# A hand-fixed issue order replaced by another: the same operations of an adaptive-norm, local-attention and token-mixer block in a different sequence, with other engines for some norms

## The chip, the core and the metric

The kernel runs on one core of a Trainium2 chip. The core has a matrix engine (PE, with its weight loads shown separately as PEld), a vector engine (DVE), a scalar engine for activations (ACT), a general engine (POOL) and a queue engine (SP) that issues the DMA transfers. Every engine works through its own list of instructions in the order in which they were issued and stops at the first one whose inputs are not there. The metric is the device time of one execution in microseconds (us). The kernel before takes 211.51 us, the median of three runs between 209.7 and 211.93.

## What is computed

One transformer-like block on `x` of 2048 rows by 512 columns, in bf16. A condition vector `c` gives six rows of 512 (shift, scale and gate for each half). The first half is a layer norm with shift and scale, a local dilated attention (32 heads of width 16; each row sees 8 rows at distance 0, 2, ... 14) and a projection. The second half is two layer norms in sequence and an MLP that mixes along the 2048 rows, not along the columns.

```python
def _A_ref(x, wqkv, wo):                     # H = 32 heads of 16, W, dil = (8, 2)
    qkv = (x @ wqkv) ...                     # q, k, v
    idx = pos[:, None] - off[None, :]        # rows s, s-2, ... s-14
    logits = jnp.einsum('bhsd,bhswd->bhsw', q, kg) * scale
    attn = _softmax(jnp.where(mask, logits, -1e9))
    return jnp.einsum('bhsw,bhswd->bhsd', attn, vg) ... @ wo
def _B_ref(x, w1, b1, w2, b2):               # F = 1792
    h = _layernorm(x)
    u = _gelu(jnp.einsum('bsd,sf->bdf', h, w1) + b1)
    return (jnp.einsum('bdf,fs->bds', u, w2) + b2) transposed
sa, ca, ga, sb, cb, gb = (silu(c) @ w_mod) in six rows
h = _layernorm(x) * (1 + ca) + sa
x = x + ga * _A_ref(h, A_wqkv, A_wo)
h = _layernorm(x) * (1 + cb) + sb
x = x + gb * _B_ref(h, B_w1, B_b1, B_w2, B_b2)
```

## The kernel before

The 2048 rows are 16 tiles of 128. They are worked in five chunks of 2, 4, 4, 4 and 2 tiles. The program first describes every operation (its engine or a choice of engines, what it reads and writes, which buffer it takes and frees), and then issues all of them in the order of one long list of names, `ORDER`. A name may carry a suffix: `:a`, `:d`, `:p` choose ACT, DVE or POOL where there is a choice, and `:q` makes a matrix operation issue its matmuls in four pieces of 32 output columns each:

```python
    def schedule(self):
        ...
        for pos, token in enumerate(ORDER.split()):
            name, *rest = token.split(":")
            if name == "fill":
                k, n = map(int, rest)     # n matmuls of 128 columns into a free bank
                ...
            o = by_name.pop(name)
            o.quad = rest == ["q"]
            assert all(d in done for d in o.deps), name
            for eng, dur, fn in o.alts:
                if rest and eng[0] == rest[0]:
                    o.eng, o.dur, o.fn = eng, dur, fn
    ...
    def mm(out, lhsT, rhs, **kw):
        if not G.quad:
            return nc.tensor.matmul(out, lhsT=lhsT, rhs=rhs, **kw)
        for j in range(0, P, 32):
            nc.tensor.matmul(out[j:j + 32], lhsT=lhsT[:, j:j + 32], rhs=rhs, tile_position=(0, j), **kw)
```

The names that matter, with `c` for a chunk and `t` for a tile:

- `ln1s t`, `rstd1_c`, `nb1_c`, `n1_t`: statistics (DVE), reciprocal deviation (ACT), bias (DVE) and the normalised tile of the first norm. `n2_t` and `h3_t` are the same for the second and third norm. Which engine does `n1_t`, `n2_t`, `h3_t` is letter `t` of the three strings `NE`.
- `wsc`: the weights of q, k, v scaled by the condition; `hT` and `xt t`: the transposed tile, by PE and a copy in the first two chunks, by a transposing DMA in the last three; `qkv c_..`: its projection; `ev`: the copy of the result out of PSUM.
- `qk c_d`: products of q and k (DVE), `red c_d`: their sum over a head (PE), `max`, `sub`, `exp`, `esum`, `rcp`, `smB`: softmax; `a2_c`: a DMA that spreads the weights, `vd c_d`: a DMA that spreads v; `pv c_d`: products of weights and v (DVE), `pvacc c_d`: their sum (PE), `oev`: its copy.
- `wo t`, `x1_t`, `ln2q t`, `ln2m`, `aff`, `ln3s`: projection, residual, sums for the second norm, shift and scale, statistics of the third.
- `mlp1_l_f_s`: first mixer product of feature tile `f` over some row tiles from `s`, `park`, `padd`, `gelu`: storing or adding a partial sum, activation; `mlp2_t` and `fin t`: second product and the output tile; `ld_`, `st_`: transfers.

The softmax and value part of one chunk, as code (cut):

```python
        for dlo in range(4):
            s_ = _Slot("big")
            ...
            add("dve", _t_tt2(NW * C), f, ..., alloc=s_, locks=True, name=f"qk{ch}_{dlo}")
            ...
            add("pe", ..., f, reads=["consts", "big_use"], frees=s_, writes=["psL"],
                name=f"red{ch}_{dlo}", tiled=True)
        ...
                add("dve", _t_tt2(8 * C), f, reads=[("a2sb", ba, jj) for jj in range(4)] + [("vD", ch, dq)],
                    frees=s_v, alloc=s_p, locks=True, name=f"pv{ch}_{dq}")
```

There are four `big` buffers, five `vD` buffers (`NVD: int = 5`) and six PSUM banks. The choice of engine for a normalised tile is made here:

```python
        alts = {"A": ("act", 0.8, lambda: nc.scalar.activation(dst, src, ACT.Identity, scale=r_, bias=n_)),
                "D": ("dve", 0.42, lambda: nc.vector.tensor_scalar(dst, src, args[0], args[1], op0=args[2], op1=args[3])),
                "P": ("pool", 0.8, lambda: nc.gpsimd.tensor_scalar(dst, src, args[0], args[1], op0=args[2], op1=args[3]))}
        G.add_any([alts[e]], reads=reads, writes=writes, name=name, locks=True)
```

The small numbers in these calls belong to the program's own planning; they are not measurements.

Of the kernel before, what the change touches and what calls it, by code (L numbers as in the profile page):

```python
# [182 lines left out]
act_table ld_x_1_2 ident ld_x_1_4 ld_x1 ld_c consts warm2 ld_x_4_14 ld_x0 ld_wmod1 ld_wqkv1 ln1s3 halo0 ld_x_2_8
fill:1:11 cps ln1s4 ld_x_2_6 ln1s1 ln1s2 ln1s0 ld_wqkv0 ln1s5 rstd1_0 silu_exp nb1_0 rstd1_1 n1_1 n1_0 silu_dve
ld_wmod0 ln1s15 ld_x_3_10 fill:2:83 modcols1 tr0_0 nb1_1 a1col ln1s14 n1_4 n1_5 ld_wqkv2 wsc1_3:a wsc1_2:d n1_3
hT0_2:d hT0_1:d hT0_3:a ln1s9 wsc1_1:a n1_2 ld_x_3_12 ln1s6 wsc1_0:a ld_wo3 fill:4:39 tr1_0 hT0_0:a tr1_2 ln1s7
hT1_0:a ld_wmod3 qkv0_10 wsc0_3:a wsc0_0:d ld_wmod4 hT1_1:d qkv0_12:q ln1s8 wsc0_1:a hT1_3:d rstd1_2 modcols0
wsc0_2:d ev0_12:d qkv0_00 sab nb1_2 hT1_2:d n1_6 n1_8 qvb0 n1_7 ln1s10 qkv0_02 rstd1_4 ev0_10:a wsc2_3 nb1_4
qvb_cp0 ln1s11 qkv1_10 ev0_00:a wsc2_2 ln1s13 qkv1_00 wsc2_1:a qk0_0 ev0_02:a qvb1 qkv1_12 wsc2_0:a qvb_cp1
qk0_1 ev1_10:a qkv0_22 qk0_3 qkv0_20 ev0_22:a red0_0 qk0_2 ev1_00:a xt6 qkv1_01:q ev0_20:a qk1_0 qkv1_02:q  # L190
ld_wmod2 n1_9 red0_1 vd0_0 halo_v1:a red0_2 ev1_02:a red0_3 mask qkv1_21:q ev1_12:a xt9 max0 ev1_01:a qkv1_11:q
qk1_2 ev1_21:a vd0_1 sub0:q qkv1_03:q ev1_11:a vd0_3 exp0 qkv1_13 xt7 qk1_1 esum0 ev1_13:a qkv1_22 xt8 rcp0
ev1_03:a modcol2 smB0 qkv1_20 qk1_3 a2_0_1 qkv1_23 a2_0_2 ev1_20:a a2_0_0 n1_15 red1_0 a2_0_3 red1_1 ln1s12
ev1_22:a red1_2 ld_wo1 mcols0 red1_3 rstd1_3 vd0_2 qkv2_00 nb1_3 max1 mrowt0 n1_10 n1_12 qkv2_10 ev1_23:a xt10
pv0_0 ev2_00:a qkv2_03 n1_13 pv0_3 vd1_3 qkv2_01 ev2_10:a vd1_2 n1_11 sub1 qk2_0 qkv2_12 exp1 xt11 qkv2_11
ev2_01:a ld_b2 pvacc0_0 mrows0:a pv0_2 ev2_11:a esum1 xt12 qkv2_13 rcp1 qk2_1 ev2_12:a qkv2_23 vd1_0 ev2_03:a
xt13 qkv2_20:q ev2_13:a ev2_23:a smB1 pvacc0_2 halo_k3:a qkv2_21:q qk2_3 a2_1_2 qkv2_02:q a2_1_0 red2_0 ev2_02:a
red2_1 a2_1_3 pv0_1 halo_v2:a pvacc0_3 ev2_21:a qkv3_11:q a2_1_1 st_row0 oev0_2:a ld_wo2 qk2_2 qkv3_00:q
ev2_20:a vd1_1 qkv3_02:q ld_wo0 qkv2_22:q ld_row0 ev3_02:a pv1_3 n1_14 red2_2 red2_3 ev2_22:a xt14 pvacc0_1
qkv3_01:q max2 qkv3_10:q ld_b1 ld_wmod5 pv1_1 qkv3_20:q ev3_10:a vd2_3 ev3_01:a sub2:q vd2_1 ev3_20:a qkv3_13:q  # L200
exp2 pv1_2 vd2_2 qkv3_21:q xt15 esum2:q ev3_21:a oev0_0:a qkv3_12:q pv1_0 vd2_0 ev3_13:a pvacc1_3 ev3_12:a woq_s
qkv3_23:q ev3_00:a rcp2 qkv3_22:q ev3_11:a pvacc1_2 ev3_23:a qk3_1 wo1:q pvacc1_0 x1_1 wo0:q smB2 qkv4_20:q
qk3_0 a2_2_2 oev1_3:a halo_v3:a a2_2_1 oev1_2:a pvacc1_1 a2_2_0 qkv3_03:q oev1_1:a oev1_0:a a2_2_3 qk3_2 modcol3
x1_0 ld_w1_0_512 ev3_03:a wo2:q ev4_20:a qk3_3 ln2q1 wo3:q ev3_22:a red3_0 vd3_3 x1_3 red3_1 mcols1 pv2_0 wo5:q
ln2q0 x1_2 mrowt1 wo4:q ln2q2 ln2m0 mrows1:a pv2_1 qkv4_22:q ln2q3 st_row1 vd3_0 rstd2_0 red3_2 x1_4 red3_3
warm3 ev4_22:a nb2_0 max3 n2_0 pvacc2_0 n2_1 ld_row1 qkv4_00 vd3_2 ln2m2 ln2q4 pv2_3 sub3 ld_w1_0_896 rstd2_2
pvacc2_1 exp3 x1_5 esum3:q pv2_2 ev4_00:a qkv4_02 oev2_1:a qkv4_10:q ln2q5 aff0 rcp3 pvacc2_3 oev2_0:a pvacc2_2
nb2_2 ev4_02:a smB3 qkv4_12 n2_2 ln2m4 a2_3_0 ln3s0 oev2_3:a oev2_2:a ld_w1_0_0 n2_3 ln3s1 ev4_10:a a2_3_1 wo8
halo_v4:p aff2 rstd3_0 a2_3_2 rstd2_4 wo9 a2_3_3 ev4_12:a nb3_0 nb2_4 wo7 x1_8 ln3s2 n2_5 vd4_2 warm0 n2_4 ln3s3
h3_1 ld_w2_0 aff4 rstd3_2 vd3_1 biascols h3_0 warm1 wo6:q nb3_2 biascols_cp:d ln3s4 h3_3 h3_2 x1_7 ln3s5  # L210
mlp1_0_5_0:q pv3_0 ld_w2_2 mlp1_0_2_0:q ln2q8 ln2q7 mlp1_0_6_0:q rstd3_4 x1_6 mlp1_0_0_0:q nb3_4 pv3_3 vd4_1
h3_5 mlp1_0_1_0:q h3_4 x1_9 mlp1_0_0_4:q mlp1_0_1_4:q pv3_2 vd4_3 park0_0:a pvacc3_3 mlp1_0_2_4:q park0_1:a
mlp1_0_3_0:q park0_2:a mlp1_0_3_4:q pv3_1 pvacc3_2 ln2q9 oev3_3:a ld_w1_0_1152 mlp1_0_4_0:q vd4_0 ln2q6 pvacc3_0
oev3_2:a mlp1_0_4_4:q qk4_2 oev3_0:a pvacc3_1 mlp1_0_6_4:q ld_w2_3 oev3_1:a ln2m6 mlp1_0_5_4:q qk4_0 park0_3:a
wo12:q rstd2_6 park0_4:a nb2_6 qk4_1 wo10:q n2_8 n2_7 n2_9 wo13:q ld_w1_0_1408 qk4_3 n2_6 red4_0 park0_5:a
red4_1 aff6 wo11:q x1_12 x1_13 red4_2 red4_3 x1_11 mlp1_0_10_0:q x1_10 max4 mlp1_0_9_0:q ln2q11 ln3s6 sub4:q
mlp1_0_7_0 ln3s7 exp4 ln2q12 ln3s8 esum4 mlp1_0_8_0 ln3s9 rcp4 park0_6:a mlp1_0_11_0 smB4 rstd3_6 ln2m11 a2_4_2
ln2q13 h3_7 mlp1_0_12_0 h3_6 a2_4_0 ln2m12 mlp1_0_10_4 h3_9 rstd2_12 a2_4_3 nb2_12 h3_8 a2_4_1 mlp1_0_8_4 n2_12
ln2m13 aff12 mlp1_0_8_8 rstd2_13 mlp1_0_11_4 ln2q10 nb2_13 ln3s12 n2_13 mlp1_0_7_4 ln2m10 pv4_0 rstd2_10
mlp1_0_7_8 rstd3_12 mlp1_0_9_4 ld_w1_0_1664 park0_7:a pv4_2 mlp1_0_9_8 park0_8:a mlp1_0_10_8 nb2_10 pv4_3  # L220
mlp1_0_11_8 n2_10 ld_w1_1_0 mlp1_0_12_4 rstd2_11 pv4_1 park0_9:a mlp1_0_12_8:q park0_10:a pvacc4_2 ld_w1_1_640
pvacc4_0 aff13 pvacc4_3 park0_11:a mlp1_0_13_0:q oev4_2:a ln3s13 inj1_2:q park0_12:a pvacc4_1 mlp1_0_13_4 nb2_11
aff10 rstd3_13 n2_11 ld_w2_5 oev4_0:a nb3_13 mlp1_0_13_8 wo14 nb3_12 ln3s10 aff11 rstd3_10 wo15 h3_12 x1_14
h3_13 inj1_1 ln3s11 inj1_4 mlp1_1_4_6 x1_15 ld_w1_1_896 inj1_3 mlp1_1_3_6 nb3_10 ln2s15 inj1_0 mlp1_1_0_6 h3_10
ln2s14 rstd2_15 rstd3_11 rstd2_14 n2_15 park0_13:a mlp1_1_1_6 aff15 mlp1_1_0_10 n2_14 mlp1_1_3_10 mlp1_1_4_10
park1_0:a nb3_11 ln3s15 mlp1_1_2_6 h3_11 aff14 mlp1_1_1_10 rstd3_15 mlp1_1_2_10 inj1_6 mlp1_1_6_6 nb3_15
ld_w1_1_1408 ln3s14 h3_15 mlp1_1_6_10 park1_1:d rstd3_14 inj1_5 mlp1_1_5_6 h3_14 park1_2:a mlp1_1_5_10 park1_3:d
mlp1_1_10_10 ld_w1_2_0 park1_4:a mlp1_1_8_10 park1_5:d park1_6:a mlp1_1_9_10 ld_w2_1 mlp1_1_12_10 mlp1_1_7_10
padd1_12 padd1_10 gelu12 mlp1_2_4_11 ld_w1_2_640 padd1_7 gelu10 mlp1_2_4_14 padd1_9 gelu7 mlp1_2_1_11 padd2_4
mlp1_2_2_11 ld_w2_7 padd1_8 mlp1_2_2_14 mlp1_2_3_11 gelu8 gelu4 mlp1_2_3_14 mlp1_2_0_11 padd2_3 mlp1_2_6_11  # L230
padd2_2 gelu3 gelu2 mlp1_2_0_14 padd2_6 mlp1_2_1_14 padd2_0 mlp1_2_5_11 padd2_1 mlp1_2_5_14 gelu0 mlp1_1_13_10
ld_w2_9 padd2_5 gelu1 gelu6 mlp1_1_11_10 gelu5 padd1_13 gelu13 mlp2_0_0 padd1_11 gelu9 gelu11 mlp2_0_0b mlp2_1_0
ld_w2_11 mlp2_0_0c fin1_0 mlp2_2_0 ld_w2_4 st_out1_0 mlp2_6_0 fin2_0 mlp2_5_0 mlp2_9_0 fin5_0 st_out5_0
st_out2_0 ld_w2_13 mlp2_7_0 fin9_0 fin6_0 mlp2_3_0 st_out6_0 mlp2_4_0 fin3_0 fin0_0 st_out3_0 st_out9_0
mlp2_13_0 st_out0_0 fin4_0 mlp2_8_0 fin7_0 st_out7_0 mlp2_10_0 st_out4_0 ld_w2_15 mlp2_11_0 fin10_0 fin13_0
fin8_0 mlp2_12_0 st_out13_0 fin11_0 st_out8_0 st_out10_0 st_out11_0 mlp2_14_0 fin12_0 st_out12_0 mlp2_15_0
fin14_0 mlp2_15_1 st_out14_0 fin15_0 mlp2_15_2 fin15_1 st_out15_0 st_out15_1 fin15_2 st_out15_2
"""


# [777 lines left out]
```

## Time and profile before

| | before |
|---|---|
| median of three runs | 211.51 us |
| span of the profiled execution | 208.9 us |
| PE busy | 196.4 us, 2208 matmuls |
| DVE busy | 165.3 us, 262 instructions |
| ACT busy | 113.8 us, 264 instructions |
| POOL busy | 16.9 us, 41 instructions |
| DMA moved | 35.99 MB |

Read "busy" as the time in which an instruction of the engine was under way. For PE that is generous: matmuls overlap in a pipeline, and one of 512 columns is listed with 379 ns while such matmuls start 0.22 us apart. All issues go through helpers, so the profile puts nearly all of them on one source line (L133), and instructions have to be told apart by the tiles they write and read: `big<-q_sb,k_f` is `qk`, `big<-a2sb,vD` is `pv`, `psS<-h,wst` is `mlp1`, `psS<-gT,...` is `mlp2`, `psL<-big,group` is `red`, `hT<-h` is a transposing DMA.

### The profile page before, as it was taken

To read this page: it belongs to the slowest core of one execution; us is meant where nothing else is said; L and a number is where in the kernel's file an instruction comes from. 1 tells how busy PE (TensorE), PEld (TensorE's weight loads), DVE (VectorE), ACT (ScalarE), POOL (GpSimd) and SP (SyncE) were. 2 spreads that over 40 slices of the span, in tenths; PEclk is the share of its full clock that TensorE was granted. 3 is DMA by queue.
4 is the path that set the end of the run, shared out by engine and by line. 5 is a ranking of instruction groups with operands and counts; after the bars stand their busy time and mean duration, and the time that the engine had idled before them with its cause. 6 is when DMAs were issued, how large, how long until landed. Compare 5 with 4: busy or idle time off the path is not lost.

```text
span 208.9 us, 5321 instructions
## 1 busy us (share of the span) xinstructions
PE 196.4 (94%) x2208; PEld 110.4 (53%) x2208; DVE 165.3 (79%) x262; ACT 113.8 (54%) x264; POOL 16.9 (8%) x41
## 2 busy tenths in 40 slices
PE   7999999995999898997899999999999999999993
...
DVE  3999999799999899999999999992771416370964
...
GB/s 165 341 369 259 22 199 163 175 237 140 205 155 291 153 217 263 147 230 292 122 259 136 19 78 310 232 109 246 227 348 109 28 0 119 132 75 141 25 100 52
DMA packets 55115, 35.99 MB, mean 172 GB/s; under 512 B 24628, under 2 KB 52404, under 8 KB 55092
## 3 DMA queue, kind: packets, MB, share of 16 engines
...
q10 hardware_dynamic: 8, 0.00, 0.0%
...
## 4 chain that ended last, share of the span: by engine, by line
PE 52%; DVE 28%; DMA 7%; ACT 5%; issue 4%; SPq 3%; DVEq 0%
PE psS L133 50%; DVE big L133 11%; DVE st L133 6%; DVE h L133 5%; DMA hT<-h 3%; SPq L133 3%; PE psL L133 3%; DVE mv L133 3%; DMA woq<-in_A_wo_dram 2%; DMA xx<-in_A_x_dram 2%; ACT xx L133 1%; DVE lsb L133 1%; ACT q_sb L133 1%; DVE nb L133 1%; DVE hT L133 1%
## 5 line engine op out<-in xcount | busy, mean ns | idle before, releaser
L133 PE MATMUL psS<-h,wst 128*32 128x512 bf16 (+1 forms) x392 | 51.5, 379 | 2.0 <-ACT h L133 1.6
L133 PE MATMUL psS<-hT,w_qkv 128*32 128x512 bf16 (+3 forms) x588 | 46.9, 346 | 4.0 <-DMA hT<-h 3.4
L133 PEld LDWEIGHTS <-wst 128*128 128x128 bf16 (+1 forms) x494 | 29.8, 98 | 31.8 <-issue 4.1
L133 PEld LDWEIGHTS <-w_qkv 128*32 128x32 bf16 (+1 forms) x630 | 31.3, 109 | 23.4 <-issue 7.1
L133 DVE TENSOR_TENSOR big<-a2sb,vD 128x4096 bf16<-128x4096 bf16 (+1 forms) x20 | 36.5, 1859 | 1.2 <-DMA a2sb<-lsb 1.0
L133 DVE TENSOR_TENSOR big<-q_sb,k_f 128x4096 bf16<-128x4096 bf16 (+1 forms) x20 | 36.7, 1856 | 0.7 <-ACT q_sb L133 0.7
L133 DVE SCALAR_TENSOR_TENSOR h<-psS,bcol,rows_bc 128x512 f32<-128x512 f32 (+2 forms) x18 | 12.4, 689 | 23.6 <-PE psS L133 23.5
L133 PE MATMUL psS<-gT,big 128*128 128x512 bf16 x112 | 24.5, 379 | 0.0
L133 PEld LDWEIGHTS <-ident 128*128 128x128 bf16 (+1 forms) x315 | 16.2, 104 | 6.5 <-issue 1.9
L133 PEld LDWEIGHTS <-big 128*128 128x128 bf16 x144 | 12.0, 97 | 13.8 <-issue 0.6
L133 POOL TENSOR_SCALAR h<-xx,rs,nb 128x512 bf16<-128x512 bf16 x12 | 10.0, 834 | 111.9 <-DVE nb L133 110.9
L133 PE MATMUL psS<-woq,o_sb 128*32 128x512 bf16 (+1 forms) x196 | 16.7, 380 | 0.6 <-ACT o_sb L133 0.6
L133 ACT ACTIVATE lv<-mv,epscol 128x1 f32<-128x1 f32 (+2 forms) x25 | 7.3, 290 | 16.1 <-DVE mv L133 14.6
L133 DVE BATCH_NORM_STATS2 st<-xx 128x6 f32<-128x512 bf16 x18 | 12.1, 673 | 3.7 <-DMA xx<-in_A_x_dram 3.6
L133 DVE TENSOR_TENSOR psS<-psS,gT 128x512 f32<-128x512 f32 x14 | 9.1, 695 | 6.9 <-PE psS L133 6.9
L133 ACT ACTIVATE q_sb<-psS,qvb 128x512 bf16<-128x512 f32 (+1 forms) x20 | 11.6, 601 | 4.5 <-PE psS L133 3.9
L133 PE MATMUL psS<-ident 128*128 128x128 bf16 x169 | 12.4, 240 | 1.4 <-POOL epscol L133 1.4
L133 ACT ACTIVATE h<-xx,nb,rs 128x512 bf16<-128x512 bf16 x14 | 11.2, 811 | 3.3 <-DVE nb L133 3.3
L133 ACT ACTIVATE v_sb<-psS,qvb 128x512 bf16<-128x512 f32 (+1 forms) x20 | 11.6, 605 | 1.9 <-PE psS L133 1.8
L133 DVE TENSOR_TENSOR h<-h,xx 128x512 bf16<-128x512 f32 (+2 forms) x18 | 11.4, 633 | 1.6 <-DMA out_dram<-h 0.9
L133 ACT ACTIVATE gT<-psS,bcol 128x512 bf16<-128x512 f32 x14 | 8.9, 686 | 6.6 <-DVE psS L133 6.5
L133 DVE TENSOR_TENSOR h<-h,rows_bc 128x512 bf16<-128x512 bf16 (+2 forms) x20 | 12.2, 608 | 0.4
...
## 6 DMA issues: line engine op xcount, KB each, us to landing
...
```

Of the source, the lines that this page charges most:

```text
L133: r = fn(*a, **k)
```

## The change

The list `ORDER` is replaced by another list of the same operations, and the three strings `NE` by others. No operation is added or taken away apart from the filler matmuls (133 before, 129 after). What the list moves or re-assigns, cut to its core:

```diff
-fill:1:11 cps ... fill:2:83 modcols1 tr0_0 ... fill:4:39 tr1_0 tr1_2 ... qkv0_10
+cps ... fill:2:108 tr1_0 ... tr0_0 modcols1 ... tr1_2 ... fill:0:21 qkv0_12
-wsc1_3:a wsc1_2:d wsc1_1:a wsc1_0:a wsc0_3:a wsc0_0:d wsc0_1:a wsc0_2:d wsc2_1:a wsc2_0:a
+wsc1_3:a wsc1_2:a wsc1_1:d wsc1_0:d wsc0_3:d wsc0_0:a wsc0_1:d wsc0_2:d wsc2_1:a wsc2_0:d
-hT1_1:d hT1_3:d ev0_12:d biascols_cp:d halo_v1:a halo_v2:a halo_v4:p park1_1:d park1_2:a park1_4:a park1_5:d
+hT1_1:a hT1_3:a ev0_12:a biascols_cp:a halo_v1:p halo_v2:d halo_v4:a park1_1:a park1_2:d park1_4:d park1_5:a
 # queue order around chunk 2 and 3 (only some names)
-xt11 ld_b2 xt12 vd1_0 xt13 a2_1_2 a2_1_0 a2_1_3 a2_1_1 st_row0 ld_wo2 vd1_1 ld_wo0 ld_row0
+ld_wmod4 xt12 xt13 vd1_2 a2_1_1 xt11 a2_1_0 a2_1_2 a2_1_3 xt14 vd1_3 st_row0 ld_b1 ld_wo3 ld_wo0 ld_row0
-ld_wmod5 vd2_3 vd2_1 vd2_2 xt15 vd2_0
+vd2_1 vd2_3 ld_b2 vd2_0 ld_w1_0_0 xt15 vd2_2
 # suffix :q (four pieces) on 60 matrix operations before, 44 after:
-qkv 25, sub 3, esum 2, wo 11, mlp 18, inj 1
+qkv 12, sub 3, wo 13, mlp 16
-    NE=('PDPPAPADPAAAPAAA', 'PAPPAPAAADAPDPDD', 'APPAAADDDDPPAADA'),
+    NE=('PAAPAPAADPAAAAPA', 'APAPAPAAADADDPPA', 'APPAAADDDDDDDPAD'),
```

It is meant to let the engines wait less for each other: work that another engine needs soon goes earlier, and tiles go to the engine that is less pressed at that place. The built programs agree with the list: the PE list has 4002 entries instead of 4418, mostly because fewer operations are issued in four pieces, and the DVE list fills 244 rows instead of 251 (equal neighbours share a row there).

More of the change, by code (lines that the diff above doesn't have):

```diff
@@ L182 @@
 ORDER = """
[L183 to L237, printed above, removed]
+ld_x_1_2 ld_c ident act_table ld_x_1_4 ld_x_2_8 consts warm2 ld_x1 ld_x0 cps ld_x_4_14 ld_wmod1 ln1s3 ld_wqkv1
@@ new lines @@
+ln1s4 ld_x_2_6 ld_wqkv0 ln1s5 ln1s2 ln1s0 rstd1_1 nb1_1 ln1s1 n1_4 n1_3 ld_wmod0 ln1s9 silu_exp rstd1_0 n1_5
+n1_2 nb1_0 ln1s14 n1_0 n1_1 ld_x_3_10 fill:2:108 tr1_0 silu_dve halo0 ld_wqkv2 hT1_1:a ln1s8 tr0_0 modcols1
+hT0_0:a hT0_2:d tr1_2 hT0_1:d hT0_3:a a1col wsc1_2:a wsc1_0:d ld_x_3_12 wsc1_1:d wsc1_3:a ln1s7 hT1_0:a
+fill:0:21 qkv0_12 ln1s6 ld_wmod2 wsc0_0:a wsc0_1:d qkv0_10 ld_wmod3 wsc0_2:d wsc0_3:d hT1_3:a ln1s15 qkv0_00
+rstd1_2 nb1_2 hT1_2:d ld_wmod5 n1_9 n1_6 modcols0 n1_8 qkv1_10 ld_wo1 sab ev0_10:a ln1s10 ev0_12:a qvb0 ln1s11
@@ new lines @@
+qkv0_02 wsc2_3 qvb_cp0 wsc2_0:d ev0_00:a qvb1 ln1s13 wsc2_2 qkv1_12 wsc2_1:a qvb_cp1 qk0_1 qkv1_00 ev0_02:a
+qk0_0 ev1_10:a qkv0_22 qkv0_20 ev0_22:a qk0_3 qkv1_02 ev1_00:a xt6 qk0_2 ev0_20:a red0_0 qkv1_01:q rstd1_4 qk1_0
+halo_v1:p vd0_0 ev1_02:a red0_1 red0_2 vd0_3 red0_3 ev1_12:a mask qkv1_11 ev1_01:a xt8 max0 qkv1_22 ev1_11:a
+qk1_2 n1_7 xt9 sub0 qkv1_03 ev1_22:a qkv1_13 exp0 xt7 qk1_1 esum0 ev1_13:a qkv1_23 vd0_2 ev1_03:a rcp0 qkv1_21
+ld_wo2 ev1_23:a vd0_1 smB0 modcol2 qk1_3 ev1_21:a a2_0_2 qkv1_20 a2_0_3 red1_0 ev1_20:a a2_0_1 red1_1 red1_2
@@ new lines @@
+a2_0_0 nb1_4 mcols0 ln1s12 n1_14 n1_15 red1_3 vd1_1 qkv2_10 max1 rstd1_3 qkv2_01 ev2_10:a halo_v2:d nb1_3 pv0_3
+n1_10 qkv2_00 ev2_01:a xt10 pv0_2 qkv2_11 ev2_00:a sub1 n1_13 qk2_0 vd1_0 qkv2_23 ev2_11:a ld_wmod4 n1_12
+qkv2_03 exp1 xt12 qkv2_13 qk2_1 ev2_03:a esum1 xt13 qkv2_12:q rcp1 ev2_13:a mrowt0 smB1 pvacc0_2 n1_11 vd1_2
+qkv2_02:q qk2_3 ev2_12:a a2_1_1 pvacc0_3 red2_0 halo_k3:a xt11 ev2_02:a qkv2_20:q ev2_23:a qkv2_21 qk2_2 a2_1_0
+a2_1_2 qkv2_22:q ev2_21:a a2_1_3 ev2_20:a red2_1 xt14 pv0_1 oev0_2:a red2_2 qkv3_10 ev2_22:a pv0_0 mrows0:a
@@ new lines @@
+vd1_3 qkv3_21 st_row0 pv1_2 qkv3_01 ld_b1 ld_wo3 red2_3 ld_wo0 qkv3_02:q pv1_0 qkv3_00 ev3_21:a pvacc0_0 ld_row0
+pvacc0_1 qkv3_03 vd2_1 oev0_0:a pv1_3 vd2_3 qkv3_13 ev3_03:a ld_b2 ev3_01:a qkv3_23 vd2_0 max2 ld_w1_0_0
+qkv3_12:q ev3_23:a xt15 woq_s sub2:q ev3_12:a pvacc1_3 ev3_00:a vd2_2 pvacc1_0 pv1_1 ev3_10:a wo0:q ev3_02:a
+wo1:q x1_0 qk3_0 ev3_13:a pvacc1_1 oev1_3:a pvacc1_2 exp2 qkv3_11 oev1_1:a qk3_3 esum2 oev1_2:a modcol3 rcp2
+oev1_0:a red3_0 x1_1 smB2 qkv3_20:q ev3_11:a qk3_2 a2_2_0 ln2q1 wo5:q a2_2_2 ev3_20:a a2_2_3 wo4:q x1_5 a2_2_1
@@ new lines @@
+mcols1 halo_v3:a qk3_1 qkv3_22:q ln2q0 ld_w1_0_896 x1_4 wo3:q ev3_22:a mrowt1 ln2m0 x1_3 red3_1 pv2_1 red3_2
+rstd2_0 wo2:q mrows1:a ln2q5 st_row1 ln2q3 red3_3 nb2_0 pv2_0 n2_1 qkv4_02 x1_2 ln2q4 qkv4_20:q ld_row1 ev4_02:a
+qkv4_00 vd3_2 max3 ev4_20:a ld_w1_0_512 pvacc2_1 pv2_3 n2_0 warm1 ev4_00:a sub3:q qkv4_22:q exp3 pv2_2 pvacc2_3
+ln2q2 pvacc2_0 esum3 halo_v4:a ld_w2_4 oev2_3:a qkv4_10 vd3_0 rcp3 ln2m4 ln2m2 oev2_0:a pvacc2_2 aff0 rstd2_2
+biascols oev2_2:a oev2_1:a nb2_2 smB3 n2_3 n2_2 wo8 ln3s0 a2_3_1 ev4_22:a ln3s1 a2_3_3 warm3 rstd2_4 a2_3_2
@@ new lines @@
+wo6:q aff2 rstd3_0 vd4_0 x1_8 qkv4_12:q a2_3_0 biascols_cp:a nb3_0 ev4_10:a nb2_4 ln3s3 n2_5 n2_4 ld_w2_1 wo9:q
+ln3s2 h3_1 vd3_3 h3_0 aff4 vd3_1 warm0 rstd3_2 x1_6 wo7:q nb3_2 ln3s5 h3_3 h3_2 x1_7 ln3s4 mlp1_0_6_0:q ev4_12:a
+pv3_0 mlp1_0_1_0:q rstd3_4 ln2q7 mlp1_0_5_0:q ln2q8 mlp1_0_2_0:q nb3_4 pv3_2 vd4_3 h3_4 mlp1_0_0_0:q h3_5 x1_9
+mlp1_0_0_4:q mlp1_0_1_4:q pv3_3 vd4_1 park0_0:a mlp1_0_6_4:q pvacc3_2 park0_1:a mlp1_0_2_4:q ln2q6 mlp1_0_3_0:q
+oev3_2:a pv3_1 park0_2:a pvacc3_0 pvacc3_3 ln2q9 mlp1_0_4_0:q oev3_3:a oev3_0:a mlp1_0_3_4:q ln2m6 qk4_0
@@ new lines @@
+pvacc3_1 rstd2_6 ld_w1_0_1152 mlp1_0_5_4:q oev3_1:a vd4_2 mlp1_0_4_4:q nb2_6 qk4_1 n2_7 wo12:q n2_6 qk4_3 red4_0
+park0_3:a wo11:q ld_w1_0_1408 n2_8 n2_9 qk4_2 red4_1 x1_11 wo13:q x1_12 aff6 wo10:q x1_13 park0_4:a red4_2
+red4_3 mlp1_0_9_0:q park0_5:a ln2q13 max4 mlp1_0_10_0:q ln3s7 park0_6:a sub4:q ln3s8 mlp1_0_7_0 exp4 ln3s9 x1_10
+esum4 mlp1_0_8_0 ln3s6 rcp4 mlp1_0_11_0 smB4 rstd3_6 a2_4_3 ln2q12 h3_7 mlp1_0_12_0 h3_6 a2_4_2 ln2q10 ln2m12
+h3_9 mlp1_0_7_4 a2_4_0 rstd2_12 h3_8 ln2m13 ln2q11 a2_4_1 nb2_12 mlp1_0_8_4 n2_12 rstd2_13 aff12 mlp1_0_7_8
@@ new lines @@
+mlp1_0_8_8 ln2m10 park0_7:a nb2_13 mlp1_0_10_4 ln3s12 n2_13 ld_w1_0_1664 pv4_0 mlp1_0_11_4 rstd3_12 rstd2_10
+mlp1_0_9_4 ld_w2_3 ln2m11 pv4_2 rstd2_11 mlp1_0_12_4 park0_8:a nb2_10 nb2_11 pv4_3 mlp1_0_9_8 mlp1_0_10_8
+park0_9:a mlp1_0_13_0 ld_w1_1_0 pv4_1 n2_10 pvacc4_2 park0_10:a pvacc4_3 aff10 pvacc4_0 oev4_2:a pvacc4_1
+mlp1_0_13_4 oev4_0:a aff13 mlp1_0_12_8 n2_11 ln3s13 mlp1_0_13_8 wo15 aff11 mlp1_0_11_8 x1_15 wo14 ld_w1_1_640
+park0_11:a ln2s15 ld_w1_1_896 inj1_3 inj1_1 inj1_2 x1_14 rstd2_15 mlp1_1_1_6 park0_12:a ln2s14 inj1_0 mlp1_1_0_6
@@ new lines @@
+ln3s10 rstd2_14 park0_13:a mlp1_1_3_6 nb2_15 nb2_14 ln3s11 rstd3_13 n2_14 ld_w2_0 inj1_4 rstd3_10 mlp1_1_2_6
+mlp1_1_4_6 rstd3_11 h3_10 n2_15 aff14 mlp1_1_0_10 nb3_13 ln3s14 h3_13 mlp1_1_1_10 inj1_6 mlp1_1_6_6 aff15
+rstd3_14 park1_0:a nb3_14 mlp1_1_2_10 ln3s15 h3_14 mlp1_1_3_10 mlp1_1_4_10 mlp1_1_6_10 inj1_5 h3_12 ld_w1_1_1408
+rstd3_15 mlp1_1_5_6 h3_11 park1_1:a h3_15 mlp1_1_5_10 park1_2:d mlp1_1_10_10 ld_w1_2_0 park1_3:d mlp1_1_8_10
+park1_4:d park1_5:a mlp1_1_7_10 padd1_8 padd1_10 gelu8 mlp1_1_9_10 padd1_7 park1_6:a gelu10 mlp1_1_12_10 padd1_9
```

9 lines of the change are left out of this document (added).

## The prediction

> **What bounds the kernel now.** I read the page's busy table first, then the busy shares by slice, and then asked for stretches of 5 us.
>
> ```profile
> PE 196.4 (94%) x2208; PEld 110.4 (53%) x2208; DVE 165.3 (79%) x262; ACT 113.8 (54%) x264; POOL 16.9 (8%) x41
> ...
> PE   7999999995999898997899999999999999999993
> ...
> DVE  3999999799999899999999999992771416370964
> ```
>
> Two engines are nearly full, at different times. DVE is at 9 tenths in almost every slice until about 140 us and then loosens; PE is full from about 100 us to the end. The stretches (columns: window, its length, then busy us and count of PE, PEld, DVE, ACT, POOL, the clock, DMA share, GB/s) say which engine leads where:
>
> ```profile
> 50.00:55.00 5.00, 3.97 (x76) 2.71 (x80) 5.00 (x3) 1.44 (x3) 0.00 (x0) 1.00 0.55 160
> ...
> 65.00:70.00 5.00, 3.79 (x88) 2.51 (x84) 5.00 (x4) 1.96 (x6) 0.00 (x0) 1.00 1.16 237
> ...
> 90.00:95.00 5.00, 4.07 (x54) 2.35 (x53) 4.83 (x15) 4.07 (x12) 1.66 (x3) 1.00 0.99 284
> ...
> 115.00:120.00 5.00, 5.00 (x32) 2.39 (x31) 4.50 (x19) 3.02 (x11) 0.00 (x0) 1.00 0.10 16
> ```
>
> From 39 to 95 us PE has holes of about 1 us per stretch and DVE has none: the attention is bound by DVE. From about 100 us PE has the mixer products as a stock and stays full. The chain that ended last closes with one piece:
>
> ```profile
> 129.78 75.80 PE psS L133 x378
> ```
>
> 76 us of matmuls without a wait. So I cut the time in three: (1) DVE's way to the first mixer product at 94.63 us, (2) PE's work from there to its last matmul, near 205.6 us, (3) the last output copy and store, 3.3 us. Parts 2 and 3 can hardly shrink. PE's work after 94.63, counted as 512-column products at 0.216 us each (in the steady part matmuls start that far apart), is about 110 us; it takes 111.
>
> What DVE and PE waited for in the first part:
>
> ```profile
> PE psS L133 <- DMA hT<-h: 3.4, 2, 2.2
> ```
>
> ```profile
> DVE st L133 <- DMA xx<-in_A_x_dram: 3.6, 1, 3.6
> DVE big L133 <- DMA a2sb<-lsb: 1.0, 1, 1.0
> ...
> DVE nb L133 <- ACT rs L133: 0.8, 2, 0.6
> DVE big L133 <- ACT q_sb L133: 0.7, 1, 0.7
> ```
>
> (Columns: total us, times, longest.) PE's 3.4 us at two late transposing DMAs look like the obvious prize. They are not: DVE was busy all through both, so PE caught up behind it. DVE itself waits about 3 us in all after its first input lands at 3.6 us. That is nearly all a new order can win in part 1.
>
> **What the Trainium skill says.** "Perfetto Trace Analysis", Identifying the Most-Contended Engine: matmul busy time is a poor measure of the distance to the limit, and the most contended engine may change over time. The trace agrees: PE at 94% hides about 12 us of idle and some 9 us of filler. "TensorEngine Tiling (Array Packing)", Key Properties: changing the tiling mode drains the engine. The trace shows it:
>
> ```profile
> 32.47 1.90 PE L133 MATMUL psS<-hT,w_qkv 128*128 128x512 bf16 x8
> 34.30 1.91 PE L133 MATMUL psL<-big,group 128*32 128x512 bf16 x32
> 36.14 1.05 PE L133 MATMUL psS<-hT,w_qkv 128*128 128x512 bf16 x4
> ```
>
> Eight products should take 8 x 0.216 = 1.73 us to the next start, and it is 1.83; the 32 quarter-width ones, four side by side, also 1.73, and it is 1.84. A change of mode costs about 0.1 us. "GPSIMD Engine Reference", Specifications: GpSimd shares its SBUF interface with VectorE. The trace agrees: the same DVE norm is 0.41 us alone and 0.76 beside a POOL norm.
>
> ```profile
> 8.76 0.41 DVE L133 TENSOR_SCALAR h<-xx,rs,nb 128x512 bf16<-128x512 bf16 x1
> ...
> 17.47 0.76 DVE L133 TENSOR_SCALAR h<-xx,rs,nb 128x512 bf16<-128x512 bf16 x1
> ```
>
> "TensorE: Matmul & The Clock Gate", What's actually happening: PE starts at half clock until it has been busy some 3.4 us, which is what the fillers are for. The trace agrees by duration (20 matmuls in 2.31 us at first, then 83 in 5.71), though the granted clock reads 1.00 throughout.
>
> **The change, part by part.** Durations here are start to start, from the trace: statistics of a tile 0.79 us, a DVE norm 0.33, a scaled weight slice 0.25, a DVE copy of a transposed slice 0.33, a PSUM copy of 512 columns 0.62, `qk` or `pv` of a full chunk 2.24.
>
> *DVE ahead of the first mixer products.* I added the DVE work listed ahead of `pv3`, the first operation after the last one that those products need. Before: 94 operations, 89.3 us. Gone from there: norms 1 and 7 (-0.66), the copy `ev0_12` (-0.62), two `hT` copies (-0.66), two weight slices (-0.50), the bias columns (-0.10). New: five weight slices (+1.25), norm 8 (+0.33), `halo_v2` (+0.15). Sum -0.8 us, so 88.5. The lead is there at the first score products: 2.1 us less DVE work ahead of the second one listed, 1.0 less ahead of `qk1_0`. Of this the trace lets DVE collect only part: before, the `pv0` products waited 1.0 us for `a2sb`. In the new queue order nine transfers stand ahead of the spreads, some 0.4 us sooner done by the issue times (1.3 us for a transpose, 0.65 for a v spread). Net for part 1: -0.5 us.
>
> *DVE behind that point.* +1.3 us for h3 tiles 10, 11, 12 and 15, +0.33 for n2_11, -1.0 for n2_14, n2_15 and h3_14. DVE is loose after 140 us and these tiles are needed only from about 135 us: 0.
>
> *ACT.* Three weight slices fewer (-2.0), two `hT` copies (+0.8), one PSUM copy (+0.6), two norms more in sum (+1.6), a small one fewer: +0.9 us on 113.8. On the path 0 to +0.5, because in chunks 2 and 3 ACT already delivers just in time.
>
> *POOL.* Three norms fewer, 2.5 us, each of which could stretch a DVE instruction beside it by some tenths: -0.2 us.
>
> *PE.* Fillers 133 to 129: 4 x 0.069 = -0.3 us, in a head where PE waits for data anyway. Changes of tiling mode, counted in the list: 24 before, 34 after; all ten new ones lie before the mixer, where PE has holes: 10 x 0.1 = 1.0 us of PE, of which I put +0.3 on the path (mostly in the full stretch from 22 to 48 us). The four-piece issue itself is neutral: 84 products in four pieces are busy 20.2 us, 60 whole ones 14.5, both 0.24 us.
>
> *Queue.* Two risks. The v spread `vd1_3` needs a buffer freed by `pv0_1`, near 51.7 us, and now stands ahead of the gate row; that row and two pieces of `wo` are issued later, so `woq_s`, which DVE reaches near 61 us, may wait up to 1 us. And a 512 KB load (`ld_wmod4`) and a 786 KB one (`ld_w1_0_0`) stand ahead of transposes. I allow +0.3 us for both.
>
> Sum: -0.5 - 0.2 + 0.3 + 0.3 + 0.2 (ACT) = about +0.1 on the span. The three runs before have mean 211.0 with the profiled run at 210.64. I start from the mean rather than from the highest two, shade by a few tenths because the earlier start of the score products is the firmest of these terms, and say 210.7 us.
>
> **Rivals.** *The DMA waits were the prize:* if PE's 3.4 us count, the time falls to about 207.5. For it: they are the largest PE wait. Against: DVE was 5.00 of 5.00 busy in both stretches. *A DVE stall takes the place of the gain:* the late gate row or late softmax spreads hold DVE, everything behind shifts, and since PE cannot make it up the time becomes 213 to 215. For it: there is no slack between `a2` landing (median 3.3 us) and `pv` in chunks 1 and 2. Against: the estimates above miss by tenths only. *The head decides:* chunk 1 is now normalised before chunk 0; if an input lands late, statistics wait and all shifts by 1 us, either way.
>
> **Range and chances.** The gain is capped: DVE's waits up to the mixer are some 3 us, so below 207 needs nearly all of them gone. Losses are not capped, but each named one is about 1 us. I take 207.9 to 214.2. Faster by over 2% means under 207.3: 0.08. Slower by over 2% means over 215.7: 0.07. Within: 0.85.
>
> **What would show it.** Right: the first `psS<-h,wst` product starts at 94 to 95 us, DVE stays at 4.8 or more of 5 from 40 to 95, the time from that product to the last matmul stays 110 to 111. Steps wrong: PE holes after 100 us (then part 2 is not fixed), a DVE wait at `woq` or `big<-a2sb` over 1 us (the second rival), or a first mixer product well before 93 us (then DVE had more to win than its waits). Far wrong would be a time outside 207 to 216, which needs a wait that I have not listed.

## The result and the profile after

The changed kernel takes 208.56 us, the median of six runs between 207.8 and 209.06; six runs of the kernel before beside it have median 211.51. The ratio is 0.988, with a 95% interval of 0.9837 to 0.9924. Beside the last experiments it was timed once more: 0.9829, 0.979 to 0.9868. So it is faster by 1 to 2%, some 3 us. The prediction said 210.7 us. Beside the fillers, the list drops four bias steps of the third norm and adds three (`nb2_14`, `nb2_15`, `nb3_14`), as the new engines of those tiles need them.

The page of the kernel after, first the busy table, then the shares by slice:

```profile
PE 197.8 (96%) x2000; PEld 108.1 (52%) x2000; DVE 165.0 (80%) x262; ACT 115.5 (56%) x266; POOL 16.6 (8%) x38
...
PE   7999999998999999898999999999999999999994
...
DVE  2989999999999999999999899996471404682845
```

The busy sums hardly move: DVE 165.3 to 165.0, PE 196.4 to 197.8. What changed is where the engines stand idle: the 5 that PE had in its tenth slice is gone. The same stretches as before, in the kernel after (busy us and count of PE, PEld, DVE, ACT, POOL):

```profile
50.00:55.00 5.00, 5.00 (x47) 2.15 (x40) 5.00 (x4) 1.14 (x3) 0.00 (x0) 1.00 0.58 181
65.00:70.00 5.00, 5.00 (x118) 3.38 (x120) 5.00 (x4) 4.72 (x13) 0.00 (x0) 1.00 0.41 128
90.00:95.00 5.00, 4.45 (x81) 2.32 (x77) 4.80 (x12) 4.56 (x13) 1.89 (x3) 1.00 0.73 200
```

The first two stretches are ones in which PE had holes of 1.0 and 1.2 us; now it is full there. Its wait of 3.4 us for transposing transfers has no line any more. The matmuls that mark the parts of the prediction, in the timeline of the kernel after (start, duration):

```profile
92.22 0.60 PE L133 MATMUL psS<-h,wst 128*32 128x512 bf16 x8
93.38 4.43 PE L133 MATMUL psS<-h,wst 128*32 128x512 bf16 x76 [0.55 <-POOL h L133]
...
194.31 9.30 PE L133 MATMUL psS<-gT,wst 128*128 128x512 bf16 x70
```

The first mixer product comes at 92.22 instead of 94.63 us, 2.4 earlier. The last matmul ends at 203.61 instead of 205.57. From the first to the last it is 111.4 us, where it was 110.9: the whole gain was made ahead of the mixer, and 0.4 us of it was given back. (These two executions took 210.64 and 208.57 us, so they lie 2.1 us apart where the medians lie 3.0 apart.) So the question is how DVE came 2.4 us sooner through the attention. Busy time up to the first mixer product, before and then after:

```profile
0.00:94.63 94.63, 86.98 (x1375) 57.49 (x1376) 87.22 (x121) 67.06 (x152) 12.92 (x36) 1.00 0.74 208
```

```profile
0.00:92.22 92.22, 87.81 (x1187) 55.86 (x1191) 86.14 (x119) 69.49 (x156) 13.54 (x34) 1.00 0.75 212
```

DVE (the third of the busy times) has 87.22 - 86.14 = 1.1 us less work there, and its idle time falls from 7.41 to 6.08 us, 1.3 less. The sum is the 2.4. These are DVE's waits in that stretch after the first input, before:

```profile
36.90 0.16 DVE L133 SCALAR_TENSOR_TENSOR nb<-mv,rs 128x4 f32<-128x4 f32 x1 [0.56 <-ACT rs L133]
39.19 2.36 DVE L133 TENSOR_TENSOR big<-a2sb,vD 128x2048 bf16<-128x2048 bf16 x2 [0.99 <-DMA a2sb<-lsb]
55.59 1.22 DVE L133 TENSOR_REDUCE m<-psL 128x128 bf16<-128x1024 f32 x1 [0.16 <-PE psL L133]
72.57 2.29 DVE L133 TENSOR_TENSOR big<-q_sb,k_f 128x4096 bf16<-128x4096 bf16 x1 [0.66 <-ACT q_sb L133]
```

and after:

```profile
12.43 0.49 DVE L133 COPY hT<-psS 128x256 bf16<-128x256 bf16 x2 [0.46 <-ACT hT L133]
38.03 2.36 DVE L133 TENSOR_TENSOR big<-a2sb,vD 128x2048 bf16<-128x2048 bf16 x2 [0.23 <-DMA a2sb<-lsb]
73.54 2.29 DVE L133 TENSOR_TENSOR big<-a2sb,vD 128x4096 bf16<-128x4096 bf16 x1 [0.38 <-PE psL L133]
```

2.37 us of waits became 1.07. Three of the four old ones are gone, the largest shrank to a quarter, and two of 0.46 and 0.38 us are new. The experiments ask which part of the change does that.

### The profile page after: what moved, and what is told of

Read it like the earlier page. It is cut to its first block, busy times and chain, and to the rows that moved or that the text cites. A ratio compares the mean times of both kernels' runs of the same rounds, so it can differ in the third digit from the quotient of the medians.

```text
span 206.6 us, 4902 instructions
## 1 busy us (share of the span) xinstructions
PE 197.8 (96%) x2000; PEld 108.1 (52%) x2000; DVE 165.0 (80%) x262; ACT 115.5 (56%) x266; POOL 16.6 (8%) x38
## 4 chain that ended last, share of the span: by engine, by line
PE 32%; DVE 30%; issue 5%; ACT 2%; DVEq 0%
PE psS L133 32%; DVE big L133 14%; DVE h L133 7%; DVE st L133 5%; DVE mv L133 2%; DVE m L133 1%; ACT lv L133 1%; ACT gT L133 1%; DVE xx L133 1%; DVE lsb L133 1%; ACT rs L133 1%; DVE nb L133 0%; ACT h L133 0%; PE psL L133 0%; DVE mcols L133 0%
## 5 line engine op out<-in xcount | busy, mean ns | idle before, releaser
L133 PEld LDWEIGHTS <-w_qkv 128*32 128x32 bf16 (+1 forms) x462 | 29.7, 110 | 21.9 <-issue 4.6
L133 ACT ACTIVATE h<-xx,nb,rs 128x512 bf16<-128x512 bf16 x18 | 14.3, 808 | 1.8 <-DVE nb L133 1.8
L133 PE MATMUL psS<-ident 128*128 128x128 bf16 x165 | 12.9, 249 | 1.4 <-POOL epscol L133 1.4
L133 PEld LDWEIGHTS <-group 128*32 128x32 bf16 x288 | 7.3, 96 | 10.0 <-issue 4.5
L133 DVE TENSOR_TENSOR h<-h,rows_bc 128x512 bf16<-128x512 bf16 (+2 forms) x20 | 11.6, 586 | 0.4
```

The lines of the kernel that those rows point to most:

```text
L133: r = fn(*a, **k)
```

## Experiments

All are compared with the kernel before, timed in the same minutes on the same chip. A ratio comes from many executions and a trace from one, which can lie over 1 us off the median (experiment 4: 211.43 against 212.75 us). Theory D says that DVE's work and waits up to the mixer set the time; P that PE's two waits for transposing transfers do; E that the new engine choices bring the gain; Q that the smaller number of matmuls issued in four pieces does.

**1. One product later.** In the kernel before, `qkv4_20` stands ahead of `qkv3_03` on PE and must wait for a late transpose:

```
-... smB2 qkv4_20:q qk3_0 ... a2_2_0 qkv3_03:q oev1_1:a
+... smB2 qk3_0 ... a2_2_0 qkv3_03:q qkv4_20:q oev1_1:a
```

> The kernel before, with one move: the first projection of chunk 4 (qkv4_20, which stands waiting 1.2 us for a transposing DMA) goes behind the last projection of chunk 3 (qkv3_03). Theory D (the time is set by DVE's work and DVE's waits up to the first mixer product): the PE wait held qkv3_03, and with it DVE's wait of 0.66 us for q; that wait goes, the first mixer product comes at about 94.0 instead of 94.63 us and the time falls by about 0.6 us, ratio 0.997. Theory P (PE's own waits for the transposing DMAs, 3.4 us in all, are the gain): PE's wait there goes, 1.2 us, ratio 0.994. Theory E (other engines for some tiles are the gain): nothing, 1.000. Theory Q (fewer matmuls in four pieces are the gain): nothing, 1.000.

Measured: 0.9962 (0.9932 to 0.9992), or -0.8 us of 212.08. This is the line it aimed at, in PE's timeline of the kernel before:

```profile
68.75 1.07 PE L133 MATMUL psS<-hT,w_qkv 128*32 128x256 bf16 x32 [1.21 <-DMA hT<-h]
```

PE stands 1.21 us for the transpose, the product for chunk 3 behind it comes late, so does ACT's copy of it, and DVE waits 0.66 us at 72.57. With the one move both waits are gone from the trace. So an idle PE in a stretch where DVE reads 5.00 of 5.00 busy did cost time, one or two operations later. How much is known from the times alone: in the traced execution an input came 0.61 us late near 6 us and the spread made DVE wait 1.41 instead of 0.99 us, so its first mixer product is at 94.62, not at the 94.0 that D expected. The interval holds the ratios of both D (0.997) and P (0.994), so this run does not decide between them.

**2. The other two DVE waits taken away.** `xt7` and `xt8`, the transposes that stood right ahead of the softmax spread, go up behind `xt6`; `nb1_3`, which waits 0.56 us for ACT, goes behind `max1`:

```
-ev1_00:a xt6 qkv1_01:q ... qkv1_13 xt7 qk1_1 ... qkv1_22 xt8 ... nb1_3 max1
+ev1_00:a xt6 xt7 xt8 qkv1_01:q ... qkv1_13 qk1_1 ... qkv1_22 ... max1 nb1_3
```

> The kernel before, with two moves that touch only DVE's two waits ahead of the first value products: the transposing DMAs of tiles 7 and 8 go up in the queue, behind that of tile 6, so that they no longer stand right ahead of the four spreads of the softmax weights; and nb1_3, for which DVE waited 0.56 us, goes behind max1. Theory D: the wait of 0.99 us for a2sb falls to about 0.3 and that of 0.56 to 0; the first value product starts near 38.0 instead of 39.19 us, and the time falls by 1.0 to 1.2 us, ratio 0.995. Theory P: PE's waits at 48.9 and 67.5 us are not touched: 1.000. Theories E and Q: 1.000.

Measured: 1.0049 (1.0023 to 1.0074), slower. The DVE timeline of this run:

```profile
37.87 1.22 DVE L133 TENSOR_REDUCE m<-psL 128x128 bf16<-128x1024 f32 x1 [1.34 <-PE psL L133]
...
42.38 2.29 DVE L133 TENSOR_TENSOR big<-q_sb,k_f 128x4096 bf16<-128x4096 bf16 x1 [0.95 <-ACT k_f L133]
...
56.97 1.23 DVE L133 TENSOR_REDUCE m<-psL 128x128 bf16<-128x1024 f32 x1 [0.61 <-PE psL L133]
```

The two waits are gone as meant (1.55 us) and 2.9 us stand in other places; the first `pv` starts at 39.08 us, hardly sooner than before's 39.19. The transposes pushed a weight load back in the queue, and PE waited 1.3 us for it. The norm `n1_10`, which needs `nb1_3`, held ACT's list until that came, so a PSUM copy behind it was late.

**3. Both.** The edits of 1 and 2 together.

> The kernel before with the moves of both other runs (qkv4_20 behind qkv3_03; transposes of tiles 7 and 8 earlier; nb1_3 behind max1), all engines and suffixes as before. Theory D: the gains add, 1.6 to 1.8 us, ratio 0.992, and DVE's listed waits after the first input fall below 1 us. Theory P: 1.2 us, 0.994. Theories E and Q: 1.000.

Measured: 1.0026 (0.9994 to 1.0058), near the product of the two, 0.9962 x 1.0049 = 1.001. They add up and do not help each other.

**4. Engine choices alone.** The order of before, with the norm strings and engine suffixes of after:

```
-    NE=('PDPPAPADPAAAPAAA', 'PAPPAPAAADAPDPDD', 'APPAAADDDDPPAADA'),
+    NE=('PAAPAPAADPAAAAPA', 'APAPAPAAADADDPPA', 'APPAAADDDDDDDPAD'),
```

> The order of the kernel before with the engine choices of the changed kernel (the three norm strings and the suffixes a, d, p); the bias steps that a choice needs or makes needless are added and dropped beside their rstd. Theory D: DVE has 0.8 us less work ahead of the third chunk's value products, but the order was made for the other choices, so part of that turns into waits: 0 to 0.8 us less, ratio 0.996 to 1.000. Theory E: nearly the whole gain, 2.5 us, ratio 0.988. Theories P and Q: 1.000.

Measured: 1.0021 (1.0 to 1.0043). The first mixer product came at 93.88 us, 0.75 sooner than in before, but the second stage of the mixer began 64.1 us after it, where before has 62.4. PE's timeline of this run names the place:

```profile
142.23 15.92 PE L133 MATMUL psS<-h,wst 128*128 128x512 bf16 x72 [1.56 <-ACT h L133]
```

The `h` is the third norm of tile 14, moved from DVE to ACT, which reaches it too late in the old order. PE's waits for transposing transfers are down from 3.4 to 0.7 us in this run, and no time is gained; that already speaks against P.

**5. Order alone.** The order of after with the norm strings and suffixes of before.

> The order of the changed kernel with the engine choices of the kernel before (norm strings and suffixes; bias steps added and dropped as the choices need). Theory D (order, by way of what DVE waits for): most of the gain stays, ratio 0.990 to 0.994; the rest is DVE's 0.8 us and the queues that no longer fit. Theory E (the engine choices): 1.000. If order and choices only work together, it is at 1.000 as well, as the choices alone were (1.002).

Measured: 1.0080 (1.0048 to 1.0112). DVE waits 1.85 us for PE ahead of a `pv` at 76.51 us, and 1.2 us in three waits for ACT's `rs`; the first mixer product comes at 95.20. So theory E falls, and so does its opposite: either half alone is slower than nothing or the same, and the two halves fit only together.

**6 to 8. The new order up to a point.** Three kernels have the engine choices of after, its order up to a point, and the order of before behind it (operations already issued left out):

```
h1: order of after up to pv0_3      (38 us), then before's
h2: order of after up to woq_s      (60 us), then before's
h3: order of after up to mlp1_0_1_0 (93 us), then before's
```

> Engine choices of the changed kernel throughout; its order up to the first value product of chunk 0 (near 38 us), then every operation that is left in the order of the kernel before. Theory D by stages: the head brings 1.0 to 1.2 us of the 2.5, ratio 0.995. Theory P (PE's waits for transposing DMAs, which come at 48.9 and 67.5 us, after the cut): 1.000. Theory Q (matmuls in four pieces, most of whose difference comes after the cut): 0.999.

Measured: 0.9967 (0.9945 to 0.9989). The first `pv` starts at 36.67 without a wait, where before has 39.19. Of these 2.5 us 2.0 are left at the first mixer product (92.61), and 64.1 us follow to the second stage.

> Engine choices of the changed kernel throughout; its order up to the scaling of the projection weights by the gate (woq_s, near 60 us), then the order of the kernel before. Theory D by stages: head and chunks 1 and 2, 1.2 to 1.8 us, ratio 0.993. Theory P: the wait at 48.9 us is gone, that of 67.5 us mostly too, since its transpose is issued before the cut: 0.986 to 0.988, all of the gain. Theory Q: 0.994, in proportion.

Measured: 1.0036 (1.0018 to 1.0054), missed by both theories. There is no PE wait for a transpose in it, and the gain that P expected (0.986 to 0.988) is not there. At the seam the operations that had run ahead or behind meet the other order: DVE waits 2.7 us for ACT's `k_f`. That is a cost of cutting there, not of after's order, and it lies on top of whatever P's waits were worth; with experiment 4 it makes P unlikely as the main cause, without excluding a part.

> Engine choices of the changed kernel throughout; its order up to the second mixer product (near 93 us), then the order of the kernel before. Theory D: PE is full from there on, so what comes behind the cut brings nothing: the whole gain, ratio 0.987 to 0.990. If the order of the mixer and of the output part matters: 0.992 to 0.996.

Measured: 0.9942 (0.992 to 0.9965). The first mixer product is at 91.11 us, even sooner than in the profiled run of after, and still the time is longer than after's: the second stage begins 64.5 us behind it. So the order behind the first mixer product does matter, as the second of the two expectations had it. PE's timeline of this run shows the wait of experiment 4 in the same place:

```profile
139.83 15.92 PE L133 MATMUL psS<-h,wst 128*128 128x512 bf16 x73 [1.57 <-ACT h L133]
```

**9. Experiment 3 mended.** What experiment 2 ran into is cleared away, and the move of experiment 1 is in it:

```
+... ld_wmod2 ld_wmod3 ...                (the load goes out early)
+... xt6 xt7 xt8 ... qkv2_00 max1 nb1_3 ... ev2_00:a n1_10 xt10 ... ev2_10:a n1_13
+... qkv3_03:q qkv4_20:q ...
```

> The kernel before, with qkv4_20 behind qkv3_03 as in the first experiment, xt7 and xt8 moved up behind xt6, nb1_3 behind max1, and now also what the second experiment ran into cleared away: the load of w_mod part 2 goes out early, ahead of part 3, so that modcol2 need not wait behind the transposes, and the two ACT norms that need nb1_3 (n1_10, n1_13) stand behind the PSUM copies ev2_00 and ev2_10, so that they cannot hold ACT's queue. Theory D (DVE's waits up to the mixer set the time): DVE's waits for a2sb 1.0, rs 0.6 and q_sb 0.7 us go with nothing in their place, 2.0 us or more at the first mixer product, which comes at about 92.5 us; ratio 0.990 to 0.993. Rival (waits in full in-order queues only move): ratio 0.997 to 1.003, with a new DVE wait of 0.5 us or more on another releaser.

Measured: 1.0024 (0.9996 to 1.0052); the rival was right. In its timeline, PE first and DVE in the second fence:

```profile
52.27 5.34 PE L133 MATMUL psS<-hT,w_qkv 128*32 128x512 bf16 x64 [2.74 <-DMA a2sb<-lsb]
```

```profile
39.92 2.36 DVE L133 TENSOR_TENSOR big<-a2sb,vD 128x2048 bf16<-128x2048 bf16 x2 [1.69 <-DMA woq<-in_A_wo_dram]
...
58.51 1.22 DVE L133 TENSOR_REDUCE m<-psL 128x128 bf16<-128x1024 f32 x1 [2.35 <-PE psL L133]
```

The product at 52.27 is the one that waited for a transpose in before:

```profile
51.03 3.65 PE L133 MATMUL psS<-hT,w_qkv 128*32 128x512 bf16 x64 [2.17 <-DMA hT<-h]
```

There PE was 2.17 us late, and DVE's reduction behind it waited 0.16 us: the two chains ended within 0.2 us of each other at 55.6. Of the 2.35 us here, most is something else. The 64 matmuls took 5.34 instead of 3.65 us, because PE's granted clock fell right behind its wait (0.50 from 54 to 56 us; the row below has 6 tenths in the slice from 52.8 us):

```profile
PEclk9999999999699999999999999999999999999998
```

PE starts 1.24 us later and takes 1.69 longer, and DVE itself arrives 0.73 later: 0.16 + 1.24 + 1.69 - 0.73 = 2.36. Without the fall of the clock the wait would be some 0.7 us, an estimate from these figures; in experiment 3, with the clock at 1.00, it is 0.79 in the same place. So waits that DVE saves earlier are held up here, but by some 0.7 us. The wait for the spread at 39.9 was not removed either, though the last transpose ahead of it was sent 2 us sooner (issued by 31.4 instead of 33.3 us); the name in the brackets is the profile's guess, as that buffer is no input of the instruction. Why the transfer landed late is open.

**10. The back alone.** Choices of after; order of before up to `mlp1_0_1_0`, order of after behind it.

> The engine choices of after; the order of the kernel before up to the first mixer piece with a bias column, mlp1_0_1_0, and the order of after behind it: the mirror image of the run with after's order up to the mixer. If the order behind the mixer is worth what that run suggests (the time from the first mixer product to the second stage of the mixer was 64.5 us there and 62.8 in after, so 1.7 us): the ratio is the 1.002 of the run with engine choices alone less 0.7%, so 0.993 to 0.997, with about 62.8 us in that stretch and a first mixer product at about 94. If part 2 of the prediction is fixed and the 64.5 us were jitter: 1.000 to 1.004.

Measured: 1.0056 (1.0034 to 1.0079), missed by both. First mixer product 95.06, second stage 64.4 us later. The wait of 1.56 us for tile 14 is gone (one of 0.29 for ACT's `gT` stands there), but PE's timeline has a new one:

```profile
103.61 0.62 PE L133 MATMUL psS<-big,group 128*32 128x512 bf16 x8 [1.31 <-DVE big L133]
```

After's back part asks early for products of `pv3` that before's front delivers later. So neither back part is better in itself; each fits its own front.

**11. The four-piece form.** After in order and engine choices, but 60 operations in four pieces, as in before; 21 go from whole to four pieces and 5 the other way:

```
-qkv0_12 ... qkv1_11 ... sub0 ... qkv1_03 ... (44 operations with :q)
+qkv0_12:q ... qkv1_11:q ... sub0:q ... qkv1_03:q ... (60 operations with :q)
```

> After in order and engine choices, but each product is issued whole or in four pieces as in the kernel before. Theory Q (fewer four-piece products, 208 matmul instructions fewer, is what gains): ratio about 1.000. Theory D and the joint-order theory: the four-piece form is neutral, ratio 0.987 to 0.990, as after.

**12. After again.** Unchanged.

> After, unchanged, as the measure for the other three on the same chip in the same minutes: ratio 0.984 to 0.992 by the result. First mixer product at about 92.2 us, second stage of the mixer 62.8 us later, if the profiled run of the result was typical; with jitter in the landing of transfers of 0.6 us either way on each.

Measured: 0.9944 (0.9907 to 0.9981) for the one, 0.9829 (0.979 to 0.9868) for the other; 210.41 against 208.07 us. The intervals do not touch: with the new order in place, the form of these 26 operations is worth about 1.1% (2.3 us). That is two thirds of the 1.7% that after gains here, so both expectations missed, and mine that the form is neutral by more. After's first mixer product is at 91.45 us this time, the second stage again 62.8 us later. The same work of PE in the two traces, after again first, then with the old forms:

```profile
26.29 1.92 PE L133 MATMUL psS<-hT,w_qkv 128*128 128x512 bf16 x7
...
33.32 2.18 PE L133 MATMUL psL<-big,group 128*32 128x512 bf16 x32
```

```profile
26.96 2.05 PE L133 MATMUL psS<-hT,w_qkv 128*32 128x512 bf16 x19
...
34.59 1.91 PE L133 MATMUL psL<-big,group 128*32 128x512 bf16 x32
```

Between the two lines lie the same products: 33.32 - 26.29 = 7.03 us and 34.59 - 26.96 = 7.63. The list has two changes of tiling mode in that stretch in after and six with the old forms, so the four more cost 0.15 us each if they are all of the difference, and PE has no hole there to hide it. Behind the start of the mixer, where PE is full too, it is three changes against seven, and the time from the first product to the second stage 62.8 against 63.5 us; these 0.7 us do reach the end. In all there are 34 and 32: the number is not what counts.

The other 1.9 us, by which this run's first mixer product is late (93.32 against 91.45 us), are not shown to come from the changes. Up to there DVE waits nowhere for PE. It waits 0.94 us for an input near 8 us, and longer for the spread ahead of the first `pv`, again after first:

```profile
37.54 2.36 DVE L133 TENSOR_TENSOR big<-a2sb,vD 128x2048 bf16<-128x2048 bf16 x2 [0.48 <-DMA a2sb<-lsb]
```

```profile
39.42 2.36 DVE L133 TENSOR_TENSOR big<-a2sb,vD 128x2048 bf16<-128x2048 bf16 x2 [1.49 <-DMA a2sb<-lsb]
```

The spread was issued at nearly the same time in both (from 33.36 and 33.45 us) and came 1.9 us later with the old forms. Whether that is chance or follows from the forms is open.

## Why the prediction was right, and which of its steps were wrong

The range held the result, and the centre was 2.1 us too high. Some of that was luck: the terms added up to +0.1 us, no gain at all, and the median lies 0.7 us above the range's lower end of 207.9. The width of the range and the choice of starting point carried it, more than the terms.

- **The cut in three** held: DVE's way shrank by 2.4 us, the rest kept its length (111.4 us, inside the 110 to 111 to within 0.4). DVE read 4.8 or more of 5 from 40 to 95 us but for two stretches (4.48 from 70, 4.76 from 80 us). But "can hardly shrink" must be read with "can well grow": with another front, or other engine choices, the stretch to the second stage took 64.1 to 64.5 us instead of 62.4 to 62.8, with one PE wait of 1.3 to 1.6 us in it.
- **"DVE itself waits about 3 us in all ... nearly all a new order can win"**: the waits gave 1.3 us and the shorter work 1.1. A first mixer product "well before 93 us" was to show that DVE had more to win than its waits, and it came at 92.22. The work was in the prediction's own sum.
- **The term that was mis-sized is "Net for part 1: -0.5"**, against -2.4 measured. Of its pieces, the work of DVE was -0.8 and measured -1.1; that stood. The step that failed was to let only part of it through and to credit one wait alone. The `a2sb` wait fell by 0.76 us, the `rs` wait of 0.56 went because `nb1_3` now stands behind other work, and the `q_sb` wait of 0.66 went as well.
- **"The earlier start of the score products is the firmest of these terms"**: it did not come. These are DVE's first score products, before and then after:

```profile
21.06 1.20 DVE L133 TENSOR_TENSOR big<-q_sb,k_f 128x2048 bf16<-128x2048 bf16 x1
22.25 5.69 DVE L133 TENSOR_TENSOR big<-q_sb,k_f 128x2048 bf16<-128x2048 bf16 x4
```

```profile
21.16 6.87 DVE L133 TENSOR_TENSOR big<-q_sb,k_f 128x2048 bf16<-128x2048 bf16 x5
```

  Such products follow each other by 1.14 us, so the second starts at 22.30 instead of 22.25 us. Up to the fifth (`qk1_0`) DVE has 0.4 us less work, not 1.0, and a new wait of 0.46 us for ACT's `hT` takes it.
- **The spreads "some 0.4 us sooner done by the issue times"**: the wait shrank for another reason. The first spread was issued at 33.85 us, 0.4 later than before's 33.43, but DVE could use them 4.2 us after that and not 5.8. The prediction had nothing of the kind.
- **"They are not" the prize**: half wrong. For PE's 1.21 us at 68.75 experiment 1 shows 0.8 us (0.2 to 1.4), by way of DVE's wait at 72.57, which I had listed without following it back. The 2.17 us at 51.03 cost only 0.16 directly, but in experiments 2, 3 and 9 PE's late product there is what catches DVE when it is to gain ahead of it (0.61, 0.79 and, by the estimate, 0.7 us). Full DVE slices did not prove that PE's hole was free.
- **DVE behind the mixer, 0**: right for after as a whole. With the old order the third norm of tile 14 costs PE 1.56 us; the new order is what makes the term zero.
- **ACT, "0 to +0.5"**: its busy time rose by 1.7 us, 113.8 to 115.5, where 0.9 was worked out, and up to the mixer no new DVE wait on it is over 0.46 us. It was not the cause of a loss.
- **PE, "+0.3 on the path (mostly in the full stretch from 22 to 48 us)"**: the forms went the other way. By experiment 11 the new ones, within the new order, save some 2.3 us, of which 0.7 are traced to PE behind the first mixer product. I counted ten more mode changes and did not place them. By the traces, PE has four changes from 22 to 36.5 us in before and in after, and eight in experiment 11; from there to 48 us it has three before and five after, and behind them PE in after waits 0.53 us for DVE at 49.85, so their cost has room. The drain that the Trainium skill names in "TensorEngine Tiling (Array Packing)", Key Properties, showed again: 0.1 us a change by the trace before, 0.15 in experiment 11. "The four-piece issue itself is neutral" holds for the busy time of a product, not for the time between neighbours of different form.
- **POOL, -0.2**: its reading was wrong. The DVE norm of 0.41 us at 8.76, called alone, had a POOL norm beside it from 8.83 us; what differs at 17.47 is told in the last section.
- **Queue, +0.3**: did not come. `woq_s` started at 59.73 us without a wait, so the second rival has nothing to show.

What stays open: how the 3 us divide between order, choices and form. The parts do not add up (order alone 1.008, choices alone 1.002, both without the form 0.994, all 0.983), so no share can be given to each. And why the spread ahead of the first `pv` makes DVE wait 0 to 1.7 us in different runs was not settled: from the issue of its first part to that `pv` it takes 4.2 to 4.3 us in after, its repeat and experiments 5 to 8, and 5.8 to 6.0 in before and experiments 1, 9, 10 and 11.
